# The column mean of the weighted w_out from two running sums on VectorE and two matmuls, in a newly planned order of steps

## The chip, the cores and the metric

The kernel runs on one core of a Trainium2 chip. A core has TensorE (PE in the profile) for matrix products, VectorE (DVE), ScalarE (ACT), GpSimd (POOL) and SyncE (SP), which here issues the transfers; each engine works through its own list of instructions in order, and engines wait for each other by semaphores. The metric is the device time of one execution in microseconds (us). Three timed runs of the kernel before gave 154.05, 154.12 and 154.29 us, median 154.12 us.

## The reference

Sliding-window attention with a few global keys, for 4 batches, 8 heads, 768 positions and 64 features a head, feeds a block of two matrix products with SoLU and a layer norm between them.

```python
scores = scale * np.matmul(q, k.transpose(0, 1, 3, 2))
...
scores = np.where(keep, scores + bias, -1000000000.0)
a = np.exp(scores - np.max(scores, axis=-1, keepdims=True))
a = a / (np.sum(a, axis=-1, keepdims=True) + 1e-09)
x = np.matmul(a, v)                      # then (B*S, H*D) = 3072 x 512
h = x @ w_in                             # 3072 x 1024
solu = h * softmax(h)
mu = np.mean(solu, axis=-1, keepdims=True)
var = np.mean((solu - mu) ** 2, axis=-1, keepdims=True)
out = ((solu - mu) / np.sqrt(var + 1e-06) * g_ln) @ w_out
```

Since `mu` is the mean of a row of `solu`, subtracting it before the last product is the same as subtracting from each weighted row `g_ln[f] * w_out[f, :]` the mean of all 1024 weighted rows. So the kernel prepares one matrix, the centred weights, once, and multiplies `solu` by it. This preparation is what the change is about.

## The kernel before

The work is cut into many small steps. A table of steps is built (`step(engine, duration, ..., dependencies, function, name=...)`, class `Plan`), and a list written out by hand of numbers, `ORDER` (line 32 on), says in which order they are issued; each engine runs its own steps in the order of that list. `SLOTS` says which buffer each step takes, `ENGS` on which engine a step runs that could run on several, and `WARM` where matmuls on a constant tile (`busy16`, line 1220) are put in as a filler. No step moves at run time, but an engine goes on to its next step as soon as that step's own inputs are there, whatever other engines do.

The steps that matter here, with their lines:

- `cast_q`, `cast_k`, `cast_v`: a loaded fp32 tile becomes fp16, on VectorE (L268), ScalarE (L266) or GpSimd (L270). `turn_k`, `turn_q` (L728) transpose on TensorE, `evac_k`, `evac_q` copy the result out of PSUM.
- `scores` (L860, L874), `exp` (L882), and for batches 1 to 3 `fac` (L890): the exponentials are multiplied by a table of factors, two fp16 tiles of SBUF in, one out, on VectorE or GpSimd. There are four of these for each batch and half of the keys, one for each pair of heads.
- `av1`, `tick`, `av2` (L1053, L1043, L1063): the products with v in two phases; the `tick` on VectorE stands between them. `xT` (L1078): VectorE multiplies the result, in PSUM, by the reciprocal row sums and stores it as the input of the first big product.
- `gemm1` (L1112): one tile of 128 rows times w_in, 8 matmuls of 512 columns; `ef` (L1118, ScalarE) and `u` (L1121, VectorE) follow. It needs w_in as fp16 (`w_in_cast`).
- `gemm2` (L1193): one tile times the centred weights, 8 matmuls; it needs all eight of them. 24 tiles go through `gemm1` and `gemm2`.

The preparation of the weights, in `weights()`:

- `w_out` arrives in four transfers (L620) as fp32, 1024 rows as 8 blocks of 128 x 512.
- `gw`, 8 steps (L633 on ScalarE, L635 on GpSimd, L639 on VectorE): block j is multiplied by its column of `g_ln` and stored as fp16 in `gw_out_sb[:, j]`. Five ran on VectorE, two on GpSimd and one on ScalarE; they do not depend on each other.
- `mean` (L646): eight matmuls of a 128 x 128 matrix of 1/1024 with the eight blocks, summed in PSUM. Every row of the result is the mean.
- `centre`, 8 steps on VectorE (L650): block j of `w_out` times its column of `g_ln` minus the mean, from the fp32 `w_out` in SBUF and the mean in PSUM, written over `gw_out_sb[:, j]`.

The order of the steps around this, as the list has it before (numbers behind a name: tile for `u`, `ef`, `gemm`; batch and pair for `cast`, `turn`, `evac`; batch, half and pair for the rest; block for `gw` and `centre`):

```
VectorE: u(2) cast_q(1,1) evac_q(1,2) u(0) evac_u(2) u(1) evac_u(0) evac_k(1,3) tick gw2 gw3
         xT(0,1,1) xT(0,1,0) gw1 gw0 tick gw5 fac(1,0,1) fac(1,1,1) xT(0,1,2) evac_u(1) xT(0,1,3)
         centre x8, u(5) evac_q(2,0) ...
GpSimd:  ... gw6 cast_k(1,2) cast_k(1,3) cast_v gw7 kg kg cast_k(2,1) fac(1,0,3) fac(1,0,2) cast_v cast_q(2,1)
ScalarE: ... evac_q(1,3) exp(1,1,1) exp(1,0,1) exp(1,1,2) gexp gw4 exp(1,0,3) exp(1,0,2) sq(1) ...
TensorE: ... scores(1,0,2) scores(1,0,3) av2 mean scores(1,1,3) gscores turn_k(2,1) gemm1(5) turn_q(2,0)
         gemm1(4) sums turn_k(2,0) gemm2(2) gemm1(3) ...
```

Of the kernel before, what the change touches and what calls it, by code (L numbers as in the profile page):

```python
# [62 lines left out]
"""  # L63
SLOTS = """
# [10 lines left out]
"""  # L75
ENGS = """
# [1182 lines left out]
```

## Time and profile before

| what | value |
|---|---|
| timed runs | 154.05, 154.12, 154.29 us |
| span of the profiled execution, first to last instruction | 154.3 us |
| TensorE busy | 144.9 us, 94% |
| ScalarE busy | 123.4 us, 80% |
| VectorE busy | 119.2 us, 77% |
| GpSimd busy | 60.0 us, 39% |
| granted TensorE clock, mean | 1.000 |

The page gives the span of the profiled execution, 154.3 us, and no separate time beside it; the span stands among the three timed runs, so what lies around it is less than a run differs from the next.

The rows that the prediction shows come from five kinds of views. A table of stretches gives, for each stretch of time, its length and then the busy time of PE, PE's weight loads (PEld), DVE, ACT and POOL with the number of instructions, the clock, the share of the DMA engines and the rate of the transfers. A timeline gives start, length, engine, line, operation, output<-input, shape, count, and in brackets how long the engine sat idle before and what ended that. The view of one line gives the shortest, the median and the longest duration in ns. The groups by line give, behind the bar, the sum, the mean and the idle time before. The chain that ended last gives start, length and what. A matmul's length in a timeline includes its way through the array, so eight in a row are read by the distance of the starts.

### The profile page before, as it was taken

Reading aid. Unit: us, or ns where it says so; the run is one execution under the profiler, and the core shown is the slowest. Engines: PE = TensorE matmul, PEld = TensorE weight load, DVE = VectorE, ACT = ScalarE, POOL = GpSimd, SP = SyncE. Lnnn points to the kernel's source line nnn. Section 1 sums busy time; section 2 is a strip of 40 time slices with the busy share of each in tenths; the row PEclk is TensorE's granted clock in tenths of the full one; section 3 lists DMA queues with packets and bytes.
Section 4 is the critical chain, followed back from the end, with each engine's and each line's share of the span. In section 5 each row is a group of like instructions: output and inputs, shape, how many; then the busy total and the mean of one; then the engine's idle time right before and its main releaser. Section 6 shows DMA issues by size and latency. Waiting matters only on the chain.

```text
span 154.3 us, 4774 instructions
## 1 busy us (share of the span) xinstructions
PE 144.9 (94%) x1877; PEld 77.9 (50%) x1877; DVE 119.2 (77%) x241; ACT 123.4 (80%) x212; POOL 60.0 (39%) x145
## 2 busy tenths in 40 slices
PE   6988899999899999799999999999999999999991
PEld 2545556477554565644544644544445644444451
DVE  6749988899999994789799959399893885799200
ACT  3959999799999888499999887878885676884642
POOL 7574456565394626852813115454212000110000
PEclk9999999999999999999999999999999999999999
DMA  4999999999996997999999999998999954488743
GB/s 146 373 305 337 307 391 327 347 340 398 295 264 108 242 285 175 220 270 233 262 196 154 271 141 244 171 233 161 189 231 259 247 141 97 90 222 223 224 166 136
DMA packets 76429, 36.35 MB, mean 236 GB/s; under 512 B 65456, under 2 KB 71928, under 8 KB 76408
## 3 DMA queue, kind: packets, MB, share of 16 engines
q1 hardware_dynamic: 76120, 35.54, 95.0%
q10 hardware_dynamic: 288, 0.52, 0.9%
q8 instruction: 14, 0.23, 0.7%
q14 instruction: 7, 0.06, 0.1%
HBM read 23.15 MB, written 6.29 MB: 191 GB/s over the span
## 4 chain that ended last, share of the span: by engine, by line
PE 44%; DMA 19%; ACT 9%; DVE 8%; POOL 7%; SPq 5%; issue 5%; POOLq 0%; DVEq 0%; ACTq 0%
PE acc L1193 16%; PE acc L1112 15%; DMA v<-in_v_dram 6%; DMA x<-in_q_dram 5%; DMA qT<-x 4%; PE acc L1053 3%; DMA kT<-x 3%; SPq L486 3%; ACT eb L882 2%; POOL x L270 2%; PE acc L728 2%; PE acc L874 2%; DVE uu L1121 2%; ACT ef L1118 2%; ACT rr L1018 1%
## 5 line engine op out<-in xcount | busy, mean ns | idle before, releaser
L1112 PE MATMUL acc<-w_in_sb,xT 128*128 128x512 f16 x192 | 44.4, 379 | 0.0
L1193 PE MATMUL acc<-gw_out_sb,late 128*128 128x512 f16 (+1 forms) x200 | 44.3, 371 | 0.1
L1121 DVE SCALAR_TENSOR_TENSOR uu<-ef,acc 128x1024 f16<-128x1024 f16 x24 | 29.2, 1216 | 5.4 <-ACT ef L1118 5.0
L882 ACT ACTIVATE eb<-acc 128x896 f16<-128x896 f32 (+1 forms) x32 | 29.3, 960 | 1.8 <-PE acc L874 1.8
L1193 PEld LDWEIGHTS <-late 128*128 128x128 f16 x200 | 18.9, 98 | 21.1 <-issue 0.9
L1118 ACT ACTIVATE ef<-acc 128x1024 f16<-128x1024 f32 x24 | 24.8, 1035 | 5.8 <-PE acc L1112 5.4
L1112 PEld LDWEIGHTS <-xT 128*128 128x128 f16 x192 | 18.1, 98 | 21.3 <-issue 1.1
L270 POOL CAST x<-x 128x768 f16<-128x768 f32 x17 | 14.4, 851 | 22.8 <-DMA x<-in_q_dram 7.8
L1078 DVE TENSOR_TENSOR xT<-acc,rr 128x384 f16<-128x384 f32 x32 | 16.3, 549 | 3.6 <-ACT rr L1018 1.9
L1053 PE MATMUL acc<-eb,v 64*64 64x160 f16 (+4 forms) x448 | 16.5, 221 | 2.1 <-DVE xT L1078 1.6
L1053 PEld LDWEIGHTS <-v 64*64 64x64 f16 x448 | 12.9, 106 | 6.6 <-issue 4.3
L1128 ACT ACTIVATE sqa<-uu 128x1024 f16<-128x1024 f16 x15 | 16.1, 1071 | 0.0
L1018 ACT ACTIVATE rr<-acc 128x768 f32<-128x768 f32 x16 | 12.7, 809 | 4.1 <-DVE tick L1063 2.5
L890 DVE TENSOR_TENSOR eb<-eb,fb 128x896 f16<-128x896 f16 (+1 forms) x19 | 14.1, 769 | 0.8 <-ACT eb L882 0.8
L270 POOL CAST v<-v 128x704 f16<-128x704 f32 (+3 forms) x13 | 8.8, 685 | 10.0 <-DMA v<-in_v_dram 9.3
L1220 PE MATMUL acc<-busy 128*128 128x512 f16 x36 | 10.8, 443 | 1.5 <-DVE busy L545 1.5
L728 PE MATMUL acc<-ident,x 128*128 128x128 f16 x144 | 11.1, 220 | 0.8 <-ACT x L266 0.7
L874 PE MATMUL acc<-qT,kT 64*64 64x160 f16 (+2 forms) x384 | 11.4, 227 | 0.3 <-ACT qT L266 0.3
L1132 DVE SCALAR_TENSOR_TENSOR sqv<-uu 128x1024 f16<-128x1024 f16 x9 | 11.5, 1277 | 0.1
L890 POOL TENSOR_TENSOR eb<-eb,fb 128x960 f16<-128x960 f16 (+1 forms) x5 | 10.4, 2081 | 2.0 <-ACT eb L882 2.0
L1043 PE MATMUL acc<-eg,vgz 64*64 64x384 f16 x64 | 10.8, 324 | 0.0
L268 DVE CAST x<-x 128x768 f16<-128x768 f32 x8 | 5.6, 709 | 6.7 <-POOL slr L371 2.3
(120 smaller groups left out, 205.7 us busy)
## 6 DMA issues: line engine op xcount, KB each, us to landing
x<-in_q_dram SPq DMA_DIRECT2D x16, 384.0 KB, 6.0
x<-in_k_dram SPq DMA_DIRECT2D x16, 384.0 KB, 5.1
out_dram<-osb SPq DMA_DIRECT2D x12, 256.0 KB, 4.7
v<-in_v_dram SPq DMA_DIRECT2D x12, 192.0 KB, 4.0
out_dram<-x SPq DMA_DIRECT2D x9, 256.0 KB, 2.2
late<-in_moe_w_in_dram SPq DMA_DIRECT2D x4, 512.0 KB, 7.4
w_out<-in_moe_w_out_dram SPq DMA_DIRECT2D x4, 512.0 KB, 6.0
v<-in_v_dram SPq DMA_DIRECT2D x12, 160.0 KB, 4.0
```

The lines of the kernel that those rows point to most:

```text
L270: nc.gpsimd.tensor_copy(out=out, in_=in_)
L874: nc.tensor.matmul(out=sc[o : o + 64, par, col : col + n], lhsT=kk[r, BLK * c : BLK * c + BLK], rhs=qq[r, g0 : g0 + n], start=fresh, stop= ...
L882: ex["fn"] = (lambda ex=ex, qk=qk, gw=gw: nc.scalar.activation(out=eb[at(qk, "eb")][:, :, 0:gw], in_=big(qk)[:, :, 0:gw], func=AF.Exp, sca ...
L890: (nc.gpsimd if fx["at"] == "POOL" else nc.vector).tensor_tensor(out=e, in0=e, in1=fb[:, p, :, 0:gw], op=ALU.mult)
L1018: re["fn"] = lambda re=re, sp_=sp_, w=w: nc.scalar.activation(out=rr[at(re, "rr")][:, :, 0:w], in_=big(sp_)[:, :, 0:w], func=AF.Exp, scale ...
L1053: nc.tensor.matmul(out=o_[64 * h : 64 * h + 64, gl : gl + m], lhsT=vv[r, v_at(vi, h, c), pair, :], rhs=view(eb[at(e_own[b, gi, pair], "eb" ...
L1078: nc.vector.tensor_tensor(out=xT[at(xt_own[b], "xT")][:, p, q0:q1], in0=one(av, d)[:, 0:w], in1=rr[at(re, "rr")][:, d, 0:w], op=ALU.mult)
L1112: nc.tensor.matmul(out=ph()[:, ts(fh, 512)], lhsT=xT[at(xt_own[b], "xT")][:, j, ts(t % NA, P)], rhs=w_in_sb[:, j, ts(fh, 512)], start=(j = ...
L1118: ex["fn"] = lambda g1=g1, t=t, ph=ph: nc.scalar.activation(out=ef[at(g1, "ef")], in_=ph(), func=AF.Exp, accum_out=s0[:, t : t + 1])
L1121: u["fn"] = lambda u=u, g1=g1, t=t, ph=ph: nc.vector.scalar_tensor_tensor(out=uu[at(u, "uu")], in0=ef[at(g1, "ef")], scalar=USC, in1=ph(), ...
L1128: nc.scalar.activation(out=sqs_["ACT"], in_=uu[at(u, "uu")], func=AF.Square, scale=float(D_FF) ** 0.5, accum_out=s2[:, t : t + 1])
L1193: nc.tensor.matmul(out=one(g2)[:, 0:wd], lhsT=uT[at(el_o, "uT")][:, c, :], rhs=gw_out_sb[:, c, sl_], start=(c == 0), stop=(c == NFC - 1))
```

## The change

Only the preparation of the mean and the lists are changed.

- Blocks 0 to 3 are summed in one fp32 buffer of 512 columns, blocks 4 to 7 in another. The two buffers lie in `gw_out_sb[:, 0:4]`, seen as fp32. `gw` of blocks 0 and 4 multiplies the first block into the buffer (any of three engines; here both on ScalarE). The other six steps, now named `gwadd`, run on VectorE: `w_out` block times its column of `g_ln` plus the buffer, both operands fp32 in SBUF, each waiting for the one before it in its sum. The last of each sum is written as fp16 to `gw_out_sb[:, 4]` and `gw_out_sb[:, 5]`.
- `mean` is two matmuls instead of eight.
- `centre` is as it was.
- `ORDER`, `SLOTS` and `ENGS` are new from the first to the last entry; of `WARM`'s 36 matmuls 31 are left, all ahead of the second score step (before, nine of them stood later).

```diff
-        wr = []
-        for j in range(NFC):
-            c = step(("ACT", "DVE", "POOL"), (612, 400, 1060), 16000 + 100 * j,
-                     [w_out_st[j // 2], g_st] + bias_st + [far_st], None, name="gw")
...
+        tails = []
+        for x in range(2):
+            run_, prev_ = spare[:, D_MODEL * x : D_MODEL * x + D_MODEL], None
+            for j in range(NFC // 2 * x, NFC // 2 * x + NFC // 2):
+                done = [w_out_st[j // 2], g_st]
+                if prev_ is None:
+                    c = step(("ACT", "DVE", "POOL"), (612, 400, 1060), 16000 + 100 * j,
+                             done + bias_st + [far_st], None, name="gw")
...
                 else:
-                    nc.vector.tensor_scalar(
-                        out=o, in0=i, scalar1=s, scalar2=None, op0=ALU.mult)
-            c["fn"] = weigh
-            wr.append(c)
+                    last_ = j == NFC // 2 * x + NFC // 2 - 1
+                    o = gw_out_sb[:, NFC // 2 + x, :] if last_ else run_
+                    c = step("DVE", 600, 16000 + 100 * j, done + [prev_], lambda j=j, o=o, r=run_:
+                             nc.vector.scalar_tensor_tensor(
+                                 out=o, in0=w_out32[:, j, :], scalar=g32[:, j : j + 1], in1=r,
+                                 op0=ALU.mult, op1=ALU.add), name="gwadd")
+                prev_ = c
+            tails.append(prev_)
 
         def mean():
-            for j in range(NFC):
-                nc.tensor.matmul(out=one(hold), lhsT=onesm, rhs=gw_out_sb[:, j, :],
-                                 start=(j == 0), stop=(j == NFC - 1))
-        wm = step("PE", 1727, 25000, wr + [onesm_st, hold], mean, mode="f", name="mean", lat=210, ni=16)
+            for x in range(2):
+                nc.tensor.matmul(out=one(hold), lhsT=onesm, rhs=gw_out_sb[:, NFC // 2 + x, :],
+                                 start=(x == 0), stop=(x == 1))
+        wm = step("PE", 432, 25000, tails + [onesm_st, hold], mean, mode="f", name="mean", lat=210, ni=4)
...
 WARM = """
-25:0:16 30:2:4 37:3:2 48:5:3 59:3:2 117:7:4 156:6:5
+1:3:2 8:1:4 18:0:16 36:3:4 52:7:2 92:0:3
```

The new order of the same stretch, with the numbers read as above (`gwadd` by its block):

```
VectorE: u(2) evac_q(1,1) cast_q(1,2) u(0) evac_u(2) u(1) evac_u(0) evac_k(1,2) tick evac_k(1,3)
         xT(0,1,3) xT(0,1,2) tick gwadd1 gwadd5 xT(0,1,1) gwadd6 gwadd2 gwadd7 gwadd3 xT(0,1,0)
         fac(1,0,2) centre x8, u(4) u(5) split evac_k(2,0) ...
GpSimd:  ... cast_v fac(1,0,1) kg kg kg fac(1,0,3) cast_k(2,1) cast_q(2,1) cast_k(2,0) stats ...
ScalarE: ... exp(1,0,1) sq(0) evac_q(1,3) gw0 gw4 exp(1,1,2) exp(1,0,3) exp(1,1,1) exp(1,0,2) ...
TensorE: ... scores(1,0,3) scores(1,1,1) scores(1,0,2) gscores turn_u(1) gscores scores(1,1,3) mean
         gemm1(4) gemm1(5) turn_k(2,1) sums turn_q(2,0) turn_q(2,1) turn_k(2,0) gemm2(2) gemm1(3) ...
```

Up to the first `gemm1` TensorE has the same steps as before, in another order, and up to `gemm2(2)` the same and `turn_q(2,1)` besides. SyncE issues the same transfers up to the last part of w_in, in another order; ahead of the last part of `w_out` it issues two parts of v of batch 1 and one small transfer more than before. `cast_q(2,3)`, on VectorE before, runs on ScalarE, and its transfer is issued ahead of those of k of its group, not behind them. `evac_q(2,0)` and `evac_q(2,1)` go from VectorE to ScalarE, `evac_k(2,0)` the other way.

More of the change, by code (lines that the diff above doesn't have):

```diff
@@ L624, in weights @@
         hold = step("PE", 0, 24000, w_out_st, None, take="one", mode="", name="hold_mean")
-        wr = []
-        for j in range(NFC):
-            c = step(("ACT", "DVE", "POOL"), (612, 400, 1060), 16000 + 100 * j,
-                     [w_out_st[j // 2], g_st] + bias_st + [far_st], None, name="gw")
-            def weigh(c=c, j=j):
-                o, i, s = gw_out_sb[:, j, :], w_out32[:, j, :], g32[:, j : j + 1]
-                if c["at"] == "ACT":
-                    nc.scalar.activation(out=o, in_=i, func=AF.Copy, scale=s)
-                elif c["at"] == "POOL":
-                    nc.gpsimd.tensor_tensor(
-                        out=o, in0=i, in1=bass.AP(tensor=s.tensor, offset=s.offset, ap=[s.ap[0], [0, D_MODEL]]),
-                        op=ALU.mult)
-                else:
-                    nc.vector.tensor_scalar(
-                        out=o, in0=i, scalar1=s, scalar2=None, op0=ALU.mult)
-            c["fn"] = weigh
-            wr.append(c)
+        tails = []
@@ new lines, in weights, with first @@
+        for x in range(2):
[5 more added lines that the diff above has]
+                             done + bias_st + [far_st], None, name="gw")
+                    def first(c=c, j=j, o=run_):
+                        i, s = w_out32[:, j, :], g32[:, j : j + 1]
+                        if c["at"] == "ACT":
+                            nc.scalar.activation(out=o, in_=i, func=AF.Copy, scale=s)
+                        elif c["at"] == "POOL":
+                            nc.gpsimd.tensor_tensor(
+                                out=o, in0=i, in1=bass.AP(tensor=s.tensor, offset=s.offset, ap=[s.ap[0], [0, D_MODEL]]),
+                                op=ALU.mult)
+                        else:
+                            nc.vector.tensor_scalar(
+                                out=o, in0=i, scalar1=s, scalar2=None, op0=ALU.mult)
+                    c["fn"] = first
+                else:
+                    last_ = j == NFC // 2 * x + NFC // 2 - 1
[6 more added lines that the diff above has]
+            tails.append(prev_)
```

86 rows, old and new, of tables (ENGS, ORDER, SLOTS) are left out of this document.

## The prediction

> **What bounds the kernel now.** I read the table of stretches first, cut at three steps of TensorE: the first `gemm1`, the `mean` and the first `gemm2`.
>
> ```profile
> 27.00:41.10 14.10, 13.22 (x227) 8.73 (x226) 13.25 (x26) 13.06 (x25) 7.41 (x12) 1.00 1.07 349
> 41.10:49.10 8.00, 7.86 (x85) 3.94 (x84) 8.00 (x15) 8.00 (x14) 5.20 (x4) 1.00 0.92 206
> 49.10:64.30 15.20, 13.68 (x244) 8.24 (x243) 12.52 (x23) 11.56 (x22) 9.23 (x14) 1.00 0.89 226
> 64.30:151.30 87.00, 86.53 (x946) 43.51 (x942) 64.86 (x122) 68.28 (x123) 21.81 (x42) 1.00 0.97 201
> ```
>
> From 27.0 to 151.3 us TensorE (first pair of numbers) is the bound: of 124.3 us it idles .88 + .14 + 1.52 + .47 = 3.0. But from 41.1 to 49.1 VectorE (third) is busy 8.00 of 8.00 and ScalarE too, and from 27.0 to 41.1 VectorE lacks only .85. So around the weights two engines are full at once, and work moved from TensorE to VectorE is not moved to an idle engine.
>
> Next the timelines of TensorE and GpSimd, at the points that fix the pace.
>
> ```profile
> 26.22 0.61 POOL L270 CAST w_in_sb<-late 128x512 f16<-128x512 f32 x1 [0.18 <-DMA late<-in_moe_w_in_dram]
> 27.00 1.89 PE L1112 MATMUL acc<-w_in_sb,xT 128*128 128x512 f16 x8
> 41.17 1.89 PE L646 MATMUL acc<-gw_out_sb,onesm 128*128 128x512 f16 x8 [0.31 <-ACT gw_out_sb L633]
> 49.10 1.89 PE L1193 MATMUL acc<-gw_out_sb,late 128*128 128x512 f16 x8
> 62.65 0.26 PE L1053 MATMUL acc<-eb,v 64*64 64x160 f16 x2 [1.09 <-DVE xT L1078]
> ```
>
> The first `gemm1` starts when the last cast of w_in ends (26.22 + .61 = 26.83), which waited for its transfer. The same transfers stand ahead of that one after the change, and TensorE has the same steps ahead of the first `gemm1`, so I leave its start at 27.0, give or take .4. From here all is counted by `gemm2(2)` at 49.10, which needs all eight centred blocks.
>
> **The change, part by part.** *TensorE.* Six of eight matmuls go.
>
> ```profile
> 133.89 3.45 PE acc L1112 x16
> 53.13 0.51 PE L728 MATMUL acc<-ident,x 128*128 128x128 f16 x6
> ```
>
> Sixteen such matmuls take 3.45 us in the chain that ended last, .216 each: 6 x .216 = 1.30 us less. One `turn_q`, six matmuls, moves ahead of `gemm2(2)`; I count .34, the distance to the next start in that timeline (53.13 to 53.47). With its waits as before, TensorE could be at `gemm2(2)` at 49.10 - 1.30 + .34 = 48.1. It can't use that if the centred blocks come later.
>
> *VectorE, from `u(2)` to the last `centre`.* Its timeline, with what is removed or has a like among the added steps:
>
> ```profile
> 30.08 1.22 DVE L1121 SCALAR_TENSOR_TENSOR uu<-ef,acc 128x1024 f16<-128x1024 f16 x1 [0.62 <-ACT ef L1118]
> ...
> 36.27 0.95 DVE L268 COPY kT<-acc 128x768 f16<-128x768 f16 x1
> 37.22 0.16 DVE L1063 COPY tick<-acc 128x1 f32<-128x1 f32 x1
> 37.30 0.89 DVE L639 TENSOR_SCALAR gw_out_sb<-w_out,g 128x512 f16<-128x512 f32 x2
> 38.35 1.02 DVE L1078 TENSOR_TENSOR xT<-acc,rr 128x384 f16<-128x384 f32 x2 [0.17 <-PE acc L1053]
> 39.30 0.87 DVE L639 TENSOR_SCALAR gw_out_sb<-w_out,g 128x512 f16<-128x512 f32 x2
> 40.08 0.15 DVE L1063 COPY tick<-acc 128x1 f32<-128x1 f32 x1
> 40.15 1.00 DVE L639 TENSOR_SCALAR gw_out_sb<-w_out,g 128x512 f16<-128x512 f32 x1
> 41.07 1.18 DVE L890 TENSOR_TENSOR eb<-eb,fb 128x960 f16<-128x960 f16 x2
> 42.17 0.54 DVE L1078 TENSOR_TENSOR xT<-acc,rr 128x384 f16<-128x384 f32 x1
> 42.64 0.67 DVE L268 COPY late<-acc 128x1024 f16<-128x1024 f16 x1
> ...
> 43.70 5.34 DVE L650 SCALAR_TENSOR_TENSOR gw_out_sb<-w_out,g,acc 128x512 f16<-128x512 f32 x8
> 48.97 1.20 DVE L1121 SCALAR_TENSOR_TENSOR uu<-ef,acc 128x1024 f16<-128x1024 f16 x1
> ```
>
> Removed: five multiplications, .89 + .87 + 1.00 = 2.76; one `fac` of two, .59; `evac_u(1)`, which goes to ScalarE, .67. Added: one `evac_k` more, .95, and the six `gwadd`. No row shows a `gwadd` with two fp32 operands in SBUF. Below, it is not under the .45 of a multiplication with one operand; above, it is like `centre`, same operation and size with one operand in PSUM, 5.34 / 8 = .67. I take .67, since operation, size and scalar are those of that row: 6 x .67 = 4.02. The sum is 4.02 + .95 - 2.76 - .59 - .67 = +.95 (with .45: -.4). The start of `u(2)` stays, since it waited for `ef(2)`, behind the first `gemm1`; the steps put ahead of it on VectorE use that wait of .62. So the last `centre` ends at 48.97 + .95 = 49.9. VectorE's cover of TensorE's saving is thus already gone.
>
> *SyncE's queue.* Two parts of v more stand ahead of the last part of `w_out`.
>
> ```profile
> 30.50 2.57 SPq L620 DMA_DIRECT2D w_out<-in_moe_w_out_dram  x3
> w_out<-in_moe_w_out_dram SPq DMA_DIRECT2D x4, 512.0 KB, 6.0
> v<-in_v_dram SPq DMA_DIRECT2D x12, 192.0 KB, 4.0
> ```
>
> Before, the last part was issued by 33.07 and landed, at the median of 6.0, near 39.1. Two parts of at most 192 KB at the 349 GB/s of that stretch add 1.1: 40.2. It feeds `gwadd2` and `gwadd3`, behind three `gwadd` and an `xT` (3 x .67 + .54 = 2.6). These start near 39.0, by the sums above and below (`centre` at 43.70 + .95, less 5.7), so it is needed at 41.6 and has 1.4 us to spare. I cost it at 0; beyond that, each us is one of `mean`.
>
> *What GpSimd does meanwhile.* This is the unknown that decides.
>
> ```profile
> 52.60 1.04 POOL L508 TENSOR_TENSOR vgz<-vgn,pick 128x512 f16<-128x512 f32 x1
> 52.64 1.48 DVE L890 TENSOR_TENSOR eb<-eb,fb 128x896 f16<-128x896 f16 x1
> L890 DVE TENSOR_TENSOR eb<-eb,fb x19: 610/650/1482, 26.3 to 112.6; 128x896 f16<-128x896 f16 x11, 128x960 f16<-128x960 f16 x8
> L890 POOL TENSOR_TENSOR eb<-eb,fb x5: 1880/2074/2308, 42.0 to 99.3; 128x960 f16<-128x960 f16 x4, 128x896 f16<-128x896 f16 x1
> 41.98 4.11 POOL L890 TENSOR_TENSOR eb<-eb,fb 128x960 f16<-128x960 f16 x2 [1.11 <-ACT eb L882]
> 40.05 0.82 POOL L270 CAST x<-x 128x768 f16<-128x768 f32 x1 [2.53 <-PE acc L1053]
> 40.85 1.91 ACT L882 ACTIVATE eb<-acc 128x960 f16<-128x960 f32 x2
> 40.23 0.80 ACT L633 ACTIVATE gw_out_sb<-w_out,g 128x512 f16<-128x512 f32 x1
> ```
>
> A `fac` on VectorE, with two operands in SBUF, has a median of .65; the one that started .04 behind a GpSimd multiplication of 1.04 took 1.48: it waited until that one was done. And the multiplication of .48 at 40.15 above took 1.00 beside a GpSimd cast (40.05 to 40.87). The two `fac` of GpSimd at 41.98 harmed nothing: beside them VectorE ran mostly steps with at most one operand in SBUF, such as `centre`. After the change `fac(1,0,3)` on GpSimd, 2.07, becomes ready in the middle of the `gwadd`, which all have two operands in SBUF. Its input is the second exponential behind `gw4` on ScalarE: from the end of `gw0`, where `gwadd1` may start, .80 + 1.91 = 2.7 us. The stretch of VectorE from `gwadd1` to `fac(1,0,2)` lasts 4.02 + 2 x .54 + .59 = 5.7. GpSimd has only `fac(1,0,1)` and three short steps ahead of it and stood idle there before (1.11 at 41.98), so I expect it to start at once. If it comes between two `gwadd`, VectorE waits up to 2.07; if VectorE keeps its turn until `xT(0,1,0)`, whose other operand is in PSUM, GpSimd starts beside that and `fac(1,0,2)` waits 2.07 - .54 = 1.5. The casts behind it (.82 each) can come between the `gwadd` left: twice more, 2.07 + 2 x .82 = 3.7. Bounds 0 to 3.7; I take 1.5, which both orders cost at least. Nothing hides it: `mean`, `centre` and `gemm2(2)` stand in line behind, and TensorE is ready early.
>
> One rule speaks to this. The Trainium skill, SBUF — State Buffer, Who interferes with whom, says that a VectorE instruction with two SBUF inputs contends with a GpSimd instruction that reads SBUF and that the loser waits for a whole instruction; by that rule alone the term is not 0, and it doesn't say who wins between two instructions in a row, so both ends above remain.
>
> *After `gemm2(2)`.* The idle time between 49.1 and 64.3 came from this:
>
> ```profile
> 53.34 0.47 SPq L472 DMA_DIRECT2D x<-in_q_dram  x1
> 61.16 0.98 DVE L268 CAST x<-x 128x768 f16<-128x768 f32 x1 [2.12 <-DMA x<-in_q_dram]
> ```
>
> VectorE stood 2.12 us at `cast_q(2,3)` for a transfer issued at 53.34, and the `xT` behind it in VectorE's queue freed the PSUM banks that TensorE lacked. Now this cast is on ScalarE and its transfer ahead of two others: I take the 1.52 as gone (bounds 0 and 1.52), with `rexp(1,1)` and `cast_k(2,3)` next to be late. The moved `turn_q` gives back .34. The other lists from 64.3 on keep TensorE as the bound; I leave .47 of idle time as it is (0 to 1.5, a new stall like the 1.09 above being the measure). Of the fillers, 31 of 36 remain and all stand ahead of work; none lies behind 27.0, so they cost nothing there.
>
> **Sum, against the execution of 154.3 us.** `gemm2(2)`: 49.10 + .95 + 1.5 = 51.55, so +2.45; turn -.34; later idle time -1.52. In all +.6: 154.9 us. The median of the runs, 154.12, is .2 under that span, so I forecast 154.7 us. The 1.30 of TensorE is not in the sum: it becomes waiting ahead of `mean`.
>
> **The rivals.**
>
> *GpSimd does no harm* (the other side). If `fac(1,0,3)` on GpSimd runs outside `gwadd` and `fac(1,0,2)`, or the delay is under .9 us, where the sum turns negative, then: .95 - .34 - 1.52 = -.9, 153.2 us. With the cheap `gwadd` as well, the sum starts from -.4 in place of +.95: -2.3, 151.8 us. For it: ScalarE may be late by some us and push that `fac` into the `centre` steps. Against it: `gw0`, `gw4` and the two exponentials stand in one row, as summed.
>
> *The casts come in between as well.* 3.7 in place of 1.5: +2.8, 156.9 us. For it: at 40.15 one cast was enough to double a step. Against it: they need their transfers first.
>
> *The later stall stays*, at another step: +1.5 on the main case, 156.2 us. It is also the case in which the new order doesn't do what it says.
>
> *The clock falls.* TensorE will wait some 3 us ahead of `mean`.
>
> ```profile
> 1.50 5.52 PE L1220 MATMUL acc<-busy 128*128 128x512 f16 x16 [1.50 <-DVE busy L545]
> ```
>
> The first sixteen matmuls took 5.52, against 3.45 for sixteen later: a slow phase costs 2.1, so 156.8 us. Against it: after 1.09 idle at 62.65 nothing slowed. The Trainium skill, TensorE: Matmul & The Clock Gate, What's actually happening, has the clock halved after an idle window of about 3.4 us; no row here has so long a gap in the middle.
>
> **How the numbers follow.** Main case .42, no harm .35, casts .13, stall .07, clock .03. The main case alone has 153.7 to 155.8: .4 from the first `gemm1`, .6 between 1.5 and 2.07 of GpSimd's term, the rest from the later idle time; so a tenth of it is faster and a fifth the same. A difference under .2% (.3 us) can't be told from none here. Faster: .35 x .85 + .42 x .1 = .34; same: .35 x .1 + .42 x .2 = .12; slower: .54. For 8 in 10 the range reaches from the middle of the no-harm case's lower part, 152.4, to 156.7, near the casts' case.
>
> **What would show it.** In the new profile: the first `gemm1` at 27.0 (off by over .5: the early order matters after all); `gwadd` near .67, and one of them, or the `fac` behind, over 1.5 beside a GpSimd `fac` of 2.07; `mean` near 45 with over 2 us idle ahead of it, ended by VectorE; the first `gemm2` near 51.5; no wait for `cast_q(2,3)`. If no `gwadd` or `fac` is stretched and `gemm2(2)` is at or before 50, the main case is wrong.

## The result and the profile after

The changed kernel takes 165.71 us (median of four runs, 165.25 to 167.15) beside 154.20 us for the kernel before (154.05 to 154.95): 1.073 times as long, interval 1.067 to 1.080. The sign was forecast, the size was not: 154.7 us, and a range that ended at 156.7.

Every run also lists its span. For the kernel before a time of 154.18 stands beside a span of 152.0, for the changed one 166.08 beside 164.4. So some 2 us lie around the span, and the profiled execution of before, span 154.3, was itself about 2 us slower than the median. Span and time are not as near as the section on the time before took them to be. Profile against profile the difference is 10.1 us. In what follows the times are medians of all runs of a kernel, while ratios and intervals leave out runs that lie over 1.5% above the fastest of their kernel.

Both executions are cut at the same points: the first `gemm1`, `gemm2(2)`, the ninth and the seventeenth tile's `gemm1`, the end. Kernel before:

```profile
0.00:27.00 27.00, 23.62 (x381) 13.42 (x382) 20.58 (x60) 22.14 (x34) 16.34 (x74) 1.00 1.01 312
27.00:49.10 22.10, 21.08 (x312) 12.68 (x310) 21.25 (x39) 21.06 (x38) 12.60 (x16) 1.00 1.02 297
49.10:72.60 23.50, 21.98 (x350) 12.88 (x350) 19.93 (x37) 19.86 (x35) 12.76 (x22) 1.00 1.01 235
72.60:103.36 30.76, 30.76 (x390) 15.48 (x388) 25.27 (x44) 27.01 (x50) 13.24 (x22) 1.00 1.19 209
103.36:154.30 50.94, 47.47 (x452) 23.39 (x448) 32.19 (x65) 33.35 (x61) 5.05 (x13) 1.00 0.76 184
```

Changed kernel:

```profile
0.00:29.16 29.16, 23.26 (x377) 13.76 (x378) 18.44 (x59) 21.56 (x33) 15.97 (x73) 1.00 0.92 279
29.16:57.80 28.64, 23.28 (x311) 13.17 (x311) 26.77 (x40) 22.35 (x36) 16.46 (x25) 0.88 1.05 288
57.80:79.69 21.89, 21.33 (x347) 12.23 (x345) 17.96 (x30) 19.90 (x35) 17.79 (x24) 1.00 0.68 174
79.69:111.79 32.10, 31.06 (x389) 15.87 (x388) 28.49 (x54) 24.93 (x46) 11.47 (x16) 1.00 1.12 202
111.79:164.40 52.61, 47.64 (x455) 23.42 (x448) 31.44 (x60) 31.87 (x58) 8.87 (x19) 0.99 0.77 184
```

The differences are +2.16, +6.54, -1.61, +1.34 and +1.67, in all +10.10. The second stretch is the place to read: with six matmuls fewer TensorE is busy 23.28 us in place of 21.08, at a mean clock of .88, and it is idle 5.36 us in place of 1.02.

What happens there stands in the timelines of VectorE, GpSimd and TensorE of the changed kernel (L648 are the six `gwadd`, L900 `fac`, L656 the `mean`):

```profile
42.05 1.45 DVE L648 SCALAR_TENSOR_TENSOR gw_out_sb<-w_out,g,gw_out_sb 128x512 f32<-128x512 f32 x2
43.88 5.04 DVE L648 SCALAR_TENSOR_TENSOR gw_out_sb<-w_out,g,gw_out_sb 128x512 f32<-128x512 f32 x4
44.35 2.13 POOL L900 TENSOR_TENSOR eb<-eb,fb 128x960 f16<-128x960 f16 x1 [0.60 <-ACT eb L892]
47.04 2.56 POOL L268 CAST x<-x 128x768 f16<-128x768 f32 x2 [0.56 <-DMA x<-in_k_dram]
48.97 1.01 PE L656 MATMUL acc<-gw_out_sb,onesm 128*128 128x512 f16 x2 [2.59 <-DVE gw_out_sb L648]
49.78 6.01 PE L1122 MATMUL acc<-w_in_sb,xT 128*128 128x512 f16 x16
```

The view of L648, and from the chain that ended last the transfer of the last part of `w_out`:

```profile
L648 DVE SCALAR_TENSOR_TENSOR gw_out_sb<-w_out,g,gw_out_sb x6: 736/764/2270, 42.0 to 47.6; 128x512 f32<-128x512 f32 x4, 128x512 f16<-128x512 f32 x2
```

```profile
37.90 6.83 DMA w_out<-in_moe_w_out_dram
```

Four `gwadd` take .74 to .79 us. The fourth, from 44.76 on, takes 2.27, beside GpSimd's `fac` of 2.13, and the last, from 47.62 on, takes 1.30, beside the first of GpSimd's two casts. The last part of `w_out` lands at 37.90 + 6.83 = 44.73, just ahead of the fourth `gwadd`. TensorE waits 2.59 us for the sums. And then the sixteen matmuls of `gemm1` at 49.78 take 6.01 us. The table of stretches, microsecond by microsecond, shows why (the clock is the figure behind the five busy times):

```profile
47.00:48.00 1.00, 0.00 (x0) 0.00 (x0) 1.00 (x3) 1.00 (x2) 0.96 (x1) 0.90 1.09 352
48.00:49.00 1.00, 0.03 (x1) 0.02 (x1) 1.00 (x2) 1.00 (x2) 1.00 (x2) 0.50 1.18 276
...
54.00:55.00 1.00, 1.00 (x5) 0.41 (x4) 1.00 (x3) 1.00 (x3) 0.00 (x0) 0.69 1.28 201
```

While TensorE waits, the granted clock drops to .50, and it stays there until past 54 us, 5 us after the work is back.

### The profile page after: what moved, and what is told of

It reads as the page before. It is cut to its first block, busy times and chain, and to the rows that moved or that the text cites. A ratio compares the mean times of both kernels' runs of the same rounds, so it can differ in the third digit from the quotient of the medians.

```text
span 164.4 us, 4747 instructions
## 1 busy us (share of the span) xinstructions
PE 146.6 (89%) x1866; PEld 78.4 (48%) x1866; DVE 123.1 (75%) x240; ACT 120.6 (73%) x204; POOL 70.6 (43%) x154
## 4 chain that ended last, share of the span: by engine, by line
PE 49%; DMA 19%; SPq 10%; DVE 9%; ACT 8%; issue 4%; POOL 0%; ACTq 0%; DVEq 0%
PE acc L1203 21%; PE acc L1122 18%; DMA late<-in_moe_w_in_dram 5%; DMA w_out<-in_moe_w_out_dram 4%; DMA x<-in_q_dram 4%; PE acc L1063 4%; SPq L484 3%; DMA late<-uu 3%; DMA v<-in_v_dram 3%; DVE eb L900 3%; DVE gw_out_sb L648 3%; SPq L470 2%; ACT ef L1128 2%; SPq L618 2%; ACT sqa L1138 2%
## 5 line engine op out<-in xcount | busy, mean ns | idle before, releaser
L1122 PE MATMUL acc<-w_in_sb,xT 128*128 128x512 f16 x192 | 47.1, 394 | 0.8 <-DVE osb L1217 0.5
L1128 ACT ACTIVATE ef<-acc 128x1024 f16<-128x1024 f32 x24 | 24.7, 1028 | 11.6 <-PE acc L1122 11.5
L268 POOL CAST x<-x 128x768 f16<-128x768 f32 x17 | 17.1, 1016 | 21.2 <-PE acc L738 6.6
L268 POOL CAST v<-v 128x704 f16<-128x704 f32 (+3 forms) x22 | 13.8, 645 | 16.5 <-DMA v<-in_v_dram 16.5
L1063 PE MATMUL acc<-eb,v 64*64 64x160 f16 (+3 forms) x448 | 15.9, 221 | 1.7 <-POOL v L268 0.7
L900 DVE TENSOR_TENSOR eb<-eb,fb 128x896 f16<-128x896 f16 (+1 forms) x18 | 15.1, 870 | 0.5 <-ACT vb L1184 0.5
L1138 ACT ACTIVATE sqa<-uu 128x1024 f16<-128x1024 f16 x13 | 13.7, 1053 | 1.6 <-DVE uu L1131 1.6
L1142 DVE SCALAR_TENSOR_TENSOR sqv<-uu 128x1024 f16<-128x1024 f16 x11 | 14.0, 1275 | 0.1
L900 POOL TENSOR_TENSOR eb<-eb,fb 128x960 f16<-128x960 f16 (+1 forms) x6 | 12.0, 2007 | 4.3 <-ACT eb L892 4.3
L884 PE MATMUL acc<-qT,kT 64*64 64x160 f16 (+2 forms) x384 | 12.3, 228 | 1.2 <-DVE late L266 1.0
L1214 ACT ACTIVATE x<-acc,rstd 128x512 f32<-128x512 f32 (+1 forms) x9 | 5.9, 661 | 10.0 <-PE acc L1203 9.8
```

Of the source, the lines that this page charges most:

```text
L268: nc.gpsimd.tensor_copy(out=out, in_=in_)
L900: (nc.gpsimd if fx["at"] == "POOL" else nc.vector).tensor_tensor(out=e, in0=e, in1=fb[:, p, :, 0:gw], op=ALU.mult)
L1063: nc.tensor.matmul(out=o_[64 * h : 64 * h + 64, gl : gl + m], lhsT=vv[r, v_at(vi, h, c), pair, :], rhs=view(eb[at(e_own[b, gi, pair], "eb" ...
L1122: nc.tensor.matmul(out=ph()[:, ts(fh, 512)], lhsT=xT[at(xt_own[b], "xT")][:, j, ts(t % NA, P)], rhs=w_in_sb[:, j, ts(fh, 512)], start=(j = ...
L1128: ex["fn"] = lambda g1=g1, t=t, ph=ph: nc.scalar.activation(out=ef[at(g1, "ef")], in_=ph(), func=AF.Exp, accum_out=s0[:, t : t + 1])
L1138: nc.scalar.activation(out=sqs_["ACT"], in_=uu[at(u, "uu")], func=AF.Square, scale=float(D_FF) ** 0.5, accum_out=s2[:, t : t + 1])
```

## The experiments

My theory after the result: the running sums lengthen VectorE's chain, GpSimd's two-input steps stretch it, TensorE's wait lowers the clock, and the new order is late in its transfers. The rival: the new order costs by itself, whatever is computed.

**The two parts of the change, one at a time.** e1 is the new order with the old eight multiplications and eight matmuls. e2 is the old order with the running sums: the four transfers carry the blocks in the order of the sums, the six additions stand where VectorE's multiplications stood, the first product of one sum is GpSimd's, of the other ScalarE's.

```diff
 e2, VectorE in the old order
-gw2 gw3 xT(0,1,1) xT(0,1,0) gw1 gw0 tick gw5
+gwadd1 gwadd2 gwadd3 xT(0,1,1) xT(0,1,0) tick gwadd5 gwadd6 gwadd7
```

> The new order of all steps with the old arithmetic (eight independent weighted blocks, eight matmuls in the mean). Theory A: most of the loss is the new order: its transfers put the first gemm1 at about 29.2 us (27.0 before), and it has later waits of its own; only the wait ahead of the mean and the slow clock behind it belong to the running sums. Then the mean starts near 46, no slow clock follows, and the time is 160 to 162 us. Rival B, the running sums on VectorE alone make the loss: about 154 to 155 us. Rival C, the sums cost nothing and the order all: about 165 us.

> The old order with the new arithmetic (two running sums, two matmuls); the four transfers of w_out keep their places but bring blocks 0-1, 2-3, 4-5, 6-7 in this sequence, the first block of a sum is weighted on GpSimd and on ScalarE, six additions on VectorE stand where its multiplications stood. Theory A: VectorE has about 1.3 us more (4.0 for 2.76), TensorE 1.3 less, the first gemm1 stays at 27.0: 154 to 156 us. Rival B, the running sums make the loss: 160 us or more. Rival C: about 152.8 us, all of TensorE's saving.

Measured: e1 162.52 us, ratio to before 1.042 (1.029 to 1.054); e2 163.96 us, 1.053 (1.040 to 1.065). The time of e1 is just above theory A's 162, and for e2 rival B came true. Each half alone costs 8 to 10 us, both together 11.5: the two overlap. A trace shows one execution; e1's is the longest of its four (164.70 us). The second, fourth and fifth stretches of e1 (first block) and of e2 (second block):

```profile
28.58:55.24 26.66, 22.82 (x316) 13.60 (x316) 23.42 (x39) 22.39 (x36) 14.91 (x25) 0.94 0.99 276
...
77.21:109.78 32.57, 31.07 (x389) 15.81 (x387) 28.66 (x54) 24.92 (x46) 11.62 (x16) 1.00 1.11 201
109.78:163.00 53.22, 47.80 (x456) 23.28 (x448) 31.74 (x60) 31.68 (x58) 8.76 (x19) 1.00 0.80 182
```

```profile
28.13:58.83 30.70, 23.10 (x306) 13.38 (x304) 28.77 (x42) 21.52 (x37) 14.23 (x20) 0.83 1.00 282
...
80.50:111.21 30.71, 30.71 (x390) 15.40 (x388) 25.01 (x45) 26.97 (x50) 12.46 (x23) 1.00 1.08 202
111.21:161.80 50.59, 47.45 (x452) 23.45 (x448) 32.50 (x65) 33.32 (x61) 5.33 (x13) 1.00 0.74 176
```

Behind the ninth tile the kernels part by their order, not by their arithmetic: 30.7 and 50.6 to 50.9 us with the old lists, 32.1 to 32.6 and 52.6 to 53.2 with the new ones. That is 3 to 4.5 us, most of it idle time of TensorE, in a region where the new lists were thought to be free. The traces of the kernels below agree, as far as they keep the buffers of their lists: 30.7 to 31.6 and 50.4 to 50.8 us in e5, e10, e11 and e18, with the old lists, and 32.2 to 33.0 and 51.8 to 53.8 in e3, e4, e6 to e9 and e12, with the new ones. In the second stretch e2 loses most: 30.70 in place of 22.10.

Two things in e1 were not as theory A had them. The clock fell in its trace too (.94 in the second stretch), without running sums. And one of the old multiplications, with one tensor as input, was stretched to 1.66 us while GpSimd's `fac` ran; the six on VectorE in e1:

```profile
L639 DVE TENSOR_SCALAR gw_out_sb<-w_out,g x6: 473/480/1664, 41.3 to 47.3; 128x512 f16<-128x512 f32 x6
```

So part of the overlap with GpSimd comes with the new order, whatever is added or multiplied there.

**GpSimd beside the additions.** e3 holds GpSimd in the changed kernel: ahead of `fac(1,0,3)` it copies two numbers of the tile that holds the sums. e11 does it in e2, by a copy of two numbers that VectorE's last `fac` behind the additions writes.

```diff
 e3
+                        if key == (1, 0, 3):
+                            nc.gpsimd.tensor_copy(out=tock, in_=gw_out_sb[:, NFC // 2 : NFC // 2 + 2, 0])
 e11, behind the product of fac
+                        if key == (1, 1, 1):
+                            nc.gpsimd.tensor_copy(out=tock, in_=e[:, 0, 0:2])
```

> The changed kernel, with one tiny GpSimd copy of a column of both sums ahead of its second factor step, so that GpSimd reads nothing large while the additions run. Theory A: GpSimd's factor step and two casts stretched the last additions (5.04 us for four, one of 2.27); now each takes 0.67, the mean starts near 47 in place of 48.97, TensorE waits 0.6 in place of 2.6 ahead of it, the clock doesn't fall and the time is 161 to 162.5 us. Rival D, the last transfer of w_out at 44.8 us sets the mean: no more than 0.5 us gained in front of the mean, slow clock as before, 165 us.

> e2 (163.96 us: old lists, running sums) with GpSimd held, by a copy of two numbers, until VectorE's two factor steps behind the additions are done. In e2 GpSimd's two factor steps (43.8 to 48.2 us) stand beside an addition that took 2.37 and two factor steps that took 3.56 in place of 1.2. Theory A (this overlap is about 4 us of e2's loss, and the idle TensorE and its half clock follow from it): additions 0.75 each, factor steps 0.6 each, TensorE waits at the next gscores by under 1 us and not 2.85, time 157.5 to 160.5. Theory B (VectorE's longer chain alone is the loss): 163 to 165.

Measured: e3 162.01 us, 1.045 (1.037 to 1.053), clear of the changed kernel's interval (1.067 to 1.080). e11 158.15 us, 1.021 (1.015 to 1.028): of the 9.5 us that the sums cost in the old order 5.8 go. Both times are as theory A had them. e2's rows of VectorE (`gwadd`, then two `fac`) and GpSimd:

```profile
42.44 3.94 DVE L650 SCALAR_TENSOR_TENSOR gw_out_sb<-w_out,g,gw_out_sb 128x512 f32<-128x512 f32 x3
46.30 3.56 DVE L902 TENSOR_TENSOR eb<-eb,fb 128x960 f16<-128x960 f16 x2
43.82 4.41 POOL L902 TENSOR_TENSOR eb<-eb,fb 128x960 f16<-128x960 f16 x2 [2.28 <-ACT eb L894]
```

The same in e11, with the view of its `gwadd`:

```profile
42.39 2.33 DVE L651 SCALAR_TENSOR_TENSOR gw_out_sb<-w_out,g,gw_out_sb 128x512 f32<-128x512 f32 x3
44.63 1.19 DVE L903 TENSOR_TENSOR eb<-eb,fb 128x960 f16<-128x960 f16 x2
46.79 3.96 POOL L903 TENSOR_TENSOR eb<-eb,fb 128x960 f16<-128x960 f16 x2
L651 DVE SCALAR_TENSOR_TENSOR gw_out_sb<-w_out,g,gw_out_sb x6: 751/752/752, 38.4 to 44.0; 128x512 f32<-128x512 f32 x4, 128x512 f16<-128x512 f32 x2
```

With GpSimd behind the additions, all six of them take .75 and the two `fac` 1.19 in place of 3.56. 1.61 + 2.37 = 4.0 us are saved on VectorE, and TensorE's waits that followed shrink with them. GpSimd does its part later at no cost: beside `centre`, with one operand in PSUM, its two `fac` take 3.96. By the Trainium skill, SBUF — State Buffer, Who interferes with whom, two-input VectorE instructions contend with GpSimd's reads and the loser blocks whole instructions; these rows agree. What is left of the loss in e11 isn't told apart by an experiment. In its trace TensorE still waits 1.15 and .88 us for an `xT` and 1.35 us for the last sum, and the clock falls for some 3 us.

In e3's profiled execution, the longest of its four (165.17 us, the others 161.28 to 162.71), the copy let GpSimd go only at 50.91, and no addition took over .86. Still the clock fell and the `mean` came at 49.02 there, since the first product of a sum, on ScalarE, was late. VectorE and GpSimd in e3:

```profile
44.63 0.75 DVE L651 SCALAR_TENSOR_TENSOR gw_out_sb<-w_out,g,gw_out_sb 128x512 f32<-128x512 f32 x1 [2.10 <-ACT gw_out_sb L638]
...
50.91 0.19 POOL L903 CAST tock<-gw_out_sb 128x2 f32<-128x2 f16 x1 [8.13 <-DVE gw_out_sb L663]
```

**The clock.** e4 puts twelve matmuls on the constant tile ahead of the `mean` of the changed kernel. e5 does so in e2, ten there and ten ahead of the next `gscores`.

```diff
 e4, WARM
-1:3:2 8:1:4 18:0:16 36:3:4 52:7:2 92:0:3
+1:3:2 8:1:4 18:0:16 36:3:4 52:7:2 92:0:3 273:7:12
 e5, WARM
-25:0:16 30:2:4 37:3:2 48:5:3 59:3:2 117:7:4 156:6:5
+25:0:16 30:2:4 37:3:2 48:5:3 59:3:2 117:7:4 156:6:5 250:0:10 256:1:10
```

> The changed kernel with 12 filler matmuls (2.6 us at full clock) ahead of the mean, into its own bank. Theory A: TensorE's idle 2.6 us ahead of the mean let the clock fall; with the fillers it stays at 1.00 from 48 to 56 us, the two gemm1 behind the mean take 3.45 us in place of 5.8, and the time falls by 2.0 to 2.5 us to about 163.4. Rival E, the slow stretch comes from something else (power): the clock between 48 and 56 stays near 0.6 and the time is that of the changed kernel, 165.5.

> The lists of before with the two running sums (as in e2, 163.96 us), and ten idle matmuls on the busy tile ahead of the mean and ten ahead of the following gscores step, where e2's TensorE sat idle 2.96 and 2.85 us and its granted clock was 0.5 from 48 to 56 us. Theory A (part of e2's loss is the clock that falls in these two gaps): the clock stays 1.00, the 16 matmuls of the next gemm1 take 7.0 us and not 5.9 + 2 times 1.6, and the time is 2 to 3.5 us under e2: 160.5 to 162. Theory B (the clock falls only where TensorE has nothing to do anyway, all is VectorE's chain): within 0.7 us of e2, 163.3 to 164.7.

Measured: e4 164.47 us, 1.051 (1.041 to 1.060), below the changed kernel's interval; e5 163.98 us, 1.049 (1.040 to 1.058), no different from e2. In e4 the fillers bridge the wait, the clock stays 1.00, and the sixteen matmuls take 3.63 in place of 6.01, 2.4 us less:

```profile
44.84 2.76 PE L1232 MATMUL acc<-busy 128*128 128x512 f16 x12
47.47 0.59 PE L658 MATMUL acc<-gw_out_sb,onesm 128*128 128x512 f16 x2
47.94 3.63 PE L1124 MATMUL acc<-w_in_sb,xT 128*128 128x512 f16 x16
```

e5 tells little: its second set was to write a PSUM bank that VectorE still had to read, so it waited too, and then ran at the low clock:

```profile
49.28 4.43 PE L1232 MATMUL acc<-busy 128*128 128x512 f16 x10 [3.25 <-DVE xT L1090]
```

**The transfers of the weights.** e6 issues the four `w_out` parts ahead of loads that stood before them, e7 the four `w_in` parts among the loads of 10 to 15 us. e8 has both, e3's hold and e4's fillers.

```diff
 SyncE, e6
-q(1,2) v k(1,2) k(1,3) v v v w_out w_out w_out w_out
+w_out w_out q(1,2) v k(1,2) k(1,3) v w_out w_out v v
 SyncE, e7
-k(1,0) v v v v q(1,0) v w_in v v k(1,1) w_in w_in w_in
+w_in k(1,0) w_in v v w_in v v w_in q(1,0) v v v k(1,1)
```

> The changed kernel (165.71 us) with the four w_out transfers issued ahead of loads of q, k and v that stand before them on SyncE's queue: two ahead of the load of q's unit 6, two ahead of the v loads of batch 1. Theory A (the last w_out landing at 44.76 us starts the last three additions): the last addition's start moves 1 to 3 us ahead, the mean with it, and the time is 163 to 164.5. Theory B (VectorE reaches the additions no sooner, and the loads that now stand behind are late instead): 165.2 to 167.

> The changed kernel (165.71 us) with the four w_in transfers issued among the loads of 10 to 15 us, and not at 16.2 and 20.0 to 21.4 us. Theory A (the late landing of w_in's last parts, 28.7 us, sets the first gemm1 at 29.16 us): first gemm1 at 27 to 28, time 164 to 165. Theory B (something else is late in the new order's start, the loads of x and v that its turns and scores need): first gemm1 at 28.7 or later, time 165.3 to 167.

> The changed kernel with four repairs: w_in early, w_out early, GpSimd's last factor step held back until both sums are done, and twelve idle matmuls ahead of the mean. Theory A (transfers, the shared stretch of GpSimd and VectorE, and the fallen clock are the most of the 11.5 us): 157.5 to 160.5, first gemm1 by 28, no stretch of the clock under 0.97. Theory B (the new order itself waits longer on TensorE, whatever the transfers, as the new order with the old arithmetic did at 162.5): 161 to 164.

Measured: e6 169.62 us, 1.088 (1.076 to 1.100); e7 170.57 us, 1.101 (1.094 to 1.107); e8 169.18 us, 1.087 (1.078 to 1.097). All three are slower than the changed kernel: both theories fell. What was pushed back is needed sooner than what was pulled ahead. TensorE's rows of e6 (first) and e7:

```profile
37.38 0.51 PE L740 MATMUL acc<-ident,x 128*128 128x128 f16 x6 [1.94 <-DVE x L268]
```

```profile
26.11 0.82 PE L740 MATMUL acc<-ident,x 128*128 128x128 f16 x6 [2.89 <-DVE x L268]
...
33.98 1.89 PE L1124 MATMUL acc<-w_in_sb,xT 128*128 128x512 f16 x8
```

In e6 a turn waits 1.94 us for its q, in e7 2.89, and e7's first `gemm1` comes at 33.98, 5 us later, though no cast of w_in waits for its transfer there; the granted clock was .50 from 25 to 31 us. So earlier places for `w_in` and `w_out` are no repair: the late landing isn't a fault of their place alone, and the whole start is late.

**The start.** The changed kernel has 22 fillers ahead of its first turn, the kernel before 16. e9 takes six from the first, e10 adds six to the second.

```diff
 e9, WARM
-1:3:2 8:1:4 18:0:16 36:3:4 52:7:2 92:0:3
+1:3:2 8:1:4 18:0:10 36:3:4 52:7:2 92:0:3
 e10, WARM
-25:0:16 30:2:4 37:3:2 48:5:3 59:3:2 117:7:4 156:6:5
+25:0:22 30:2:4 37:3:2 48:5:3 59:3:2 117:7:4 156:6:5
```

> The changed kernel (165.71 us) with 16 idle matmuls ahead of the first turn, as before, in place of 22. In the changed kernel they end at 9.06 us and the first turn starts at 8.89, before at 6.86, though its x is cast by 6.87. Theory A (those six matmuls are what delays the start of the new order): first turn near 7.0, first gemm1 1 to 2 us earlier (27.2 to 28.2), time 163.5 to 164.8. Theory B (the transfers are late by themselves and set the first gemm1): first gemm1 at 28.6 or later, time 165.2 to 166.5.

> The kernel before (154.2 us) with 22 idle matmuls ahead of the first turn in place of 16; they end 2 us later, near 9.0. Theory A (the start of TensorE's work sets the time, since TensorE is the bound from then on): the first gemm1 1 to 2 us later, time 155.5 to 156.5. Theory B (the start is hidden behind transfers): 153.9 to 154.8.

Measured: e9 166.63 us, with one run at 163.29 and four from 166.3 to 167.99, so whether it gained is open; e10 155.77 us, 1.004 (1.000 to 1.008). In e9's trace TensorE waits for the cast of x instead, and by its page the clock falls in the slices from 12 to 21 us:

```profile
12.01 0.51 PE L740 MATMUL acc<-ident,x 128*128 128x128 f16 x6 [1.51 <-DVE x L268]
```

In e10 the first `gemm1` comes at 28.75, 1.75 us later, the ninth tile at 72.42 as before: in this pair of traces the late start is made up by then. So the +2.16 and the -1.61 of the changed kernel may belong together; two single executions don't show it, and the idle 1.52 us of the kernel before in that stretch are .17 in e10.

**Three repairs that leave the transfers alone.** e12 is the changed kernel with e9's fillers, a hold like e11's (`key == (1, 0, 2)`) and eight fillers ahead of the `mean`.

> The changed kernel with three repairs that leave its transfers as they are: 16 idle matmuls at the start, GpSimd's factor step held until VectorE's last one behind the additions is done, eight idle matmuls ahead of the mean. Theory A (start 2 us, overlap 1.6 us, clock 2 us of the 11.5): 158.5 to 161.5. Theory B (the three overlap or something else takes their place): 162 to 165.

Measured: 163.21 us (161.27 to 164.38), 1.050 (1.043 to 1.057). It gains 2.5 us, not the sum of its parts: 8 us remain. In its trace all six additions take .75 and the clock is 1.00 from the first `gemm1` to `gemm2(2)`, and still `gemm2(2)` comes at 55.24, with the clock at .50 from 13 to 19 us and the first `gemm1` at 29.61.

**Where in the order.** e13 to e16 splice the lists: old up to the first `gemm1` and new from there on (e13 with eight matmuls, e15 with the sums), old up to 62 us and new from there on (e14 with eight matmuls, e16 with e11's sums). Behind the cut each step takes the buffer or bank free longest. e17 is the control: e1 with this choice from 60 us on, nothing else.

```diff
 e14, ORDER
+the old list up to fac(1,1,3), then the new list's steps that are left
-the new list
```

> e1 (new order, eight matmuls, 162.5 us) with the old order's steps up to the copy ahead of the first gemm1 (about 27 us), the new order from there on. Theory A (the start of the new order costs: by 24 us 1.1 MB less had been moved, by 40 us 1.9 MB): first gemm1 near 27 to 28, time 154.5 to 157.5. Theory B (what costs stands behind the first gemm1): time 160 to 163.

> The kernel before (about 154.5 us) with the new order from 62 us on, where a cast of q that VectorE waited 2.12 us for goes to ScalarE. Theory A (the prediction's step: the idle 1.5 us of TensorE behind 62 us goes): 152.6 to 153.6. Theory B (the later order takes with new waits what it gives): 154.2 to 157.

> The changed kernel (165.7 us) with the old order's steps up to the first gemm1, all else as changed. Theory A (start and sums are two costs that add): 157.5 to 161. Theory B (the sums cost the same whatever the start, and the order's cost stands behind the first gemm1): 163.5 to 166.5.

> e11 (158.15 us: old order, sums, GpSimd held until VectorE's factor steps are done) with the new order from 62 us on. Theory A (the later order gives 1.5 us): 156 to 157.2. Theory B (it gives nothing): 157.7 to 160.

> e1 (new order, eight matmuls, 162.5 us) with the buffers and banks from about 60 us on chosen anew by the rule used in e13 to e16 (of the free ones the one free longest); 183 of 216 steps that take one get another. If the choice of buffers does no harm: 161 to 164.5, and e13 to e16 stand as tests of the order. If it does: 166 or more, with more waits behind 80 us than e1, and e13 to e16 say little of the order behind their cut.

Measured: e13 163.69 us, 1.052 (1.045 to 1.060); e14 163.49, 1.047 (1.039 to 1.054); e15 169.00 (166.39 to 169.51); e16 167.09, 1.074 (1.069 to 1.080); e17 167.03, 1.070 (1.063 to 1.078). The control is 4.5 us slower than e1, so the choice of buffers alone costs about that much, and these four say little about the order behind their cut. What can be read is only that, even so, e13 reaches `gemm2(2)` at 51.91, e1 at 55.24 and e17 at 54.51: in these traces the old start gives 2.6 to 3.3 us up to there.

**One change that the traces offered.** e18 is the kernel before with `cast_q(2,3)` put behind the two `xT` that it delayed.

```diff
 VectorE
-cast_q(2,3) xT xT
+xT xT cast_q(2,3)
```

> The kernel before with one step moved on VectorE: the cast of q's last block of batch 2, for which VectorE waited 2.12 us at 59 to 61.16 us, goes behind the two xT steps after it. If that wait is what held TensorE 1.09 us at 62.65: that wait goes, time 0.5 to 1.1 us under the kernel before beside it. If the next load takes its place: within 0.3 us of it.

Measured: 154.94 us beside 154.79, 1.001 (.997 to 1.005). The wait at 62.65 is gone from its trace, a new one of .62 stands at 89.59, and the time is the same. No kernel tried beats the one before.

## Why the prediction was wrong

- **Direction, and a part of the mechanism,** held: VectorE's chain, and GpSimd's `fac(1,0,3)` beside it, make the `mean` late. In the changed kernel one `gwadd` was stretched by 2.27 - .75 = 1.5 us beside that `fac`, the size that I took, and another by 1.30 - .75 = .55 beside the cast behind it, a part of the rival with the casts.
- **`gwadd` at .67.** The number held, my reading of its source did not. The .67 of `centre` is the distance from one start to the next; each takes .73. A `gwadd` takes .75, and where the two sums alternate, as in the changed kernel, the next starts some .67 later: in e12, with GpSimd held, four take 2.77. Where three of one sum stand in a row, as in e2 and e11, each waits for the one before, and the distance is .79. The view of `centre` before, and e12's row:

```profile
L650 DVE SCALAR_TENSOR_TENSOR gw_out_sb<-w_out,g,acc x8: 731/733/733, 43.7 to 48.3; 128x512 f16<-128x512 f32 x8
```

```profile
44.91 2.77 DVE L651 SCALAR_TENSOR_TENSOR gw_out_sb<-w_out,g,gw_out_sb 128x512 f32<-128x512 f32 x4
```

- **First `gemm1` at 27.0 +- .4, since the same transfers and steps stand ahead.** This step failed. It came at 29.16. The same set in another order is not the same start: in the first 27 to 29 us 279 GB/s were moved, not 312. The bound of .4 was too narrow as well: seven traces with the old start have it at 26.7 to 28.1 (the kernel before, e2, e5, e11, e14, e16, e18), seven with the new start at 28.1 to 29.6 (the changed kernel, e1, e3, e4, e6, e9, e12), on average 27.2 and 28.9. By e10 such a delay by itself costs .6 us at the end.
- **`w_out` costed at 0, landing at 40.2, needed at 41.6.** It landed at 44.73. I moved the landing by the bytes put ahead of it, and not by the lateness of the queue as a whole. But VectorE was itself 3 us late at the first `gwadd` (42.05, not 39.0), and the `gwadd` ahead of the one that needs this part ended at 44.62, so the landing itself cost some .2 us. That a cost of 0 came out nearly right is luck: both were late.
- **The clock, chance .03, and TensorE's waiting put at nothing.** This step failed too. The clock fell, and e4 shows 2.4 us of matmul time for it. The sum has `gemm2(2)` wait for the last `centre`, with the 1.30 of TensorE lost in a wait that costs nothing more. In the changed kernel the last `centre` ends at 55.38 and `gemm2(2)` starts at 57.80; from the `mean` on TensorE works without a gap, at a mean clock of .68:

```profile
50.04 5.34 DVE L660 SCALAR_TENSOR_TENSOR gw_out_sb<-w_out,g,acc 128x512 f16<-128x512 f32 x8
```

```profile
48.97:57.80 8.83, 8.83 (x63) 4.11 (x63) 7.55 (x12) 4.08 (x8) 2.02 (x5) 0.68 1.14 221
```

  So the path to `gemm2(2)` was TensorE at half clock, and not VectorE's `centre`. I had compared one gap, 1.09 us, with a condition of one long gap. The wait that I forecast myself, over 2 us and then 2.59, came on top of others in the microseconds before, and the clock fell about 1.4 us into it.
- **Later idle time -1.52.** The third stretch is 1.61 shorter, but e2 and e10, with the old order, are shorter there too (idle .19 and .17 us), and e18 without that wait is no faster. So it was no gain of the new order; the wait that I took off is not in every execution.
- **The other lists from 64.3 on keep TensorE as the bound.** This failed: +1.34 and +1.67 in the last two stretches, +1.8 and +2.3 in e1, and none in e2. It is a term that I put at nothing without working it out. The trace shows where: from 79.69 us to 153 TensorE of the changed kernel waits 2.6 us, .34 in the like part of the kernel before. The two longest are put down to the transfer that turns a tile for `gemm2`, and to a `u` that a `scores` step waits for (in us: in total, how often, the longest):

```profile
PE acc L1203 <- DMA late<-uu: 1.3, 1, 1.3
PE acc L870 <- DVE uu L1131: 0.7, 1, 0.7
```

  The second of them stands, at .72 or .73 us, in all nine traces that keep the new lists and their buffers, and in none with the old ones.

In the terms of the forecast: start 0, measured +2.16; to `gemm2(2)` +2.45, measured +6.54; behind it -1.86 up to the ninth tile, measured -1.61; the rest 0, measured +3.0. Sum +.6, measured +10.1. `gemm2(2)` thus came 6.25 us later than forecast (57.80, not 51.55): the last `centre` was 4.0 late (55.38, not 51.4), of which 3.05 were there at the first `gwadd`, most of it the late start, and the other 2.4 are TensorE behind it at half clock.

What stays open: what in the new start moves fewer bytes, and why the steps above come late in the new lists behind 80 us. The splices were to tell, and their buffers spoiled them.

## What to carry to other kernels

Before work goes from TensorE to VectorE, list what GpSimd does at that time: two-input steps of both in SBUF side by side cost whole instructions, here, with the old order, 4 us on VectorE and 5.8 in the time, and holding GpSimd back until VectorE turns to PSUM operands took them away. Multiplications with one tensor as input were stretched as well (to 1.00 us in the kernel before, to 1.66 in e1). A forecast wait of TensorE needs a second look at the clock, with the shorter gaps ahead of it counted. And a new order of all steps is a change of its own: here it cost 8 us with the old arithmetic, so it is to be measured alone before it is put together with another change.

## What the runs showed that I had not expected

- The clock fell without any single long gap. In e11, cut by microseconds, with TensorE busy .42, .23, .47 of each:

```profile
43.00:44.00 1.00, 0.42 (x5) 0.11 (x2) 0.93 (x3) 1.00 (x2) 0.00 (x0) 1.00 1.11 295
44.00:45.00 1.00, 0.23 (x1) 0.00 (x0) 1.00 (x2) 1.00 (x2) 0.00 (x0) 1.00 0.98 281
45.00:46.00 1.00, 0.47 (x15) 0.33 (x15) 1.00 (x3) 1.00 (x3) 0.11 (x1) 1.00 1.10 311
46.00:47.00 1.00, 0.60 (x10) 0.23 (x10) 1.00 (x3) 0.44 (x2) 1.00 (x3) 0.75 1.21 237
```

  The Trainium skill, TensorE: Matmul & The Clock Gate, What's actually happening, names an idle window of about 3.4 us as the condition; here there were matmuls in every microsecond, and 1.12 us of work in the three from 43 to 46 were too few to hold the clock. In the changed kernel TensorE worked 1.59 of the 3.41 us ahead of the fall at 47.80. In the kernel before it worked 2.11 of the 3.41 us up to the end of its wait at 62.65 and a little beyond (59.99 to 63.40), and the clock stayed at 1.00.

- Other buffers for the same steps in the same order cost 4.5 us (e17 beside e1).
- The kernels of the new order spread widely from run to run, 160.0 to 164.7 us in e1; a gain of 1 us can't be told there with four runs.
